# Another order of the first loads and first products in a fused SSM and gated-MLP kernel

## The chip, the cores and the metric

The kernel runs on one core of a Trainium2 chip. The metric is the device time of one execution in microseconds (us); lower is better.

## The reference

The input x has 2048 rows of 512 values. Each row is normalised (layer norm without scale or shift), and the normalised rows `xn` go into two branches whose results are added to x:

```python
xn = _layernorm(x, axis=-1)
return x + _A_ref(xn, ...) + _B_ref(xn, w1, w3, w2)

# A: a diagonal state-space model with 512 complex states, a scan over the 2048 rows
Bu = einsum("bld,pd->blp", x + 0j, B_bar)
h = Lam_bar * h + Bu[:, t, :]                      # for each row t
y = 2.0 * einsum("blp,dp->bld", hseq, Cmat).real + x * Dskip
# B: a gated MLP with 1792 hidden values
out = (silu(x @ w1) * (x @ w3)) @ w2
```

Inputs and output are bf16. The change touches only how the first 512 rows get into branch B.

## The kernel before

Rows are worked in four blocks of 512 (`x_blk[0..3]`), each with four row tiles of 128 (called c = 0..3 in block 0). TensorE needs xn with the features on partitions, `xnT[b]`: 4 feature tiles of 128 (`NDT` = 4; `H` = 2 is one half of the contraction) by 512 rows. For later blocks VectorE normalises and a DMA transposes. Block 0 goes another way, since everything waits for it: VectorE takes mean and variance (`stats`, L164, `aggr`, L167), ScalarE makes the reciprocal root (`rstd_act`, L171 and L172), VectorE normalises (`normed`, L192), TensorE transposes 128x128 pieces against an identity into PSUM (`turn`, L251), and ScalarE or VectorE copies them out (`put`, L256 and L258).

The MLP's first layer has 14 column tiles f of 128 for w1 and for w3. `glu_mm` (L372) multiplies one f tile by some rows over some of the four contraction tiles `dts`. For f = 0, 1, 2 of block 0 the products begin piecewise, as soon as pieces of xnT and of the weights are there: `ahead` (called at L533 to L551) writes them into the three pairs of PSUM tiles `begun`, for rows `c` to `c+n` and the contraction half `lo` or `hi`. The rest of the layer is `glu_up`. Then come the state-space inputs (`ssm_in`, L411) and the outputs (`y_out`, L488 and L493).

The order of instructions on every engine is the order in which the program writes them. Other work of VectorE is drained from a queue with a cost for each task; it lies behind the stretch that the change touches.

DMAs are issued by SyncE and by ScalarE, each on a ring of its own. Completion semaphores are handed out to the DMAs from eight in turn, and an issue that takes a used one waits until the DMA before it on that semaphore has landed. SyncE issues, in this order: rows 0 to 127, rows 128 to 255 (L77), then w1 and w3 for f = 0 to 3, each in two contraction halves of 256 KB (L95, by `load_w13(0, 4, 2)`), then larger pieces. ScalarE issues Lambda_re (L109), rows 256 to 511 (L77), Lambda_im and log_dt, 1 KB each except for the rows. The three small vectors land in `prm`, which VectorE clears first, and TensorE transposes it (L544) for `par_cols`.

`keep_warm` (L150) issues products of constants that nobody reads, into a PSUM tile that is later overwritten.

Of the kernel before, what the change touches and what calls it, by code (L numbers as in the profile page):

```python
# [16 lines left out]
P = 128  # L17
# [3 lines left out]
def kernel(  # L21
# [24 lines left out]
    nc = tc.nc  # L46
# [6 lines left out]
    CPB = TBLK // P  # L53
    NSB = TBLK // SB
    NDT = D // P
# [20 lines left out]
    def load_rows(c0, c1, eng):  # L76
        eng.dma_start(out=x_blk[0][:, c0:c1, :], in_=xv[:, 0, c0:c1, :])  # L77
# [4 lines left out]
    w1_sb = const.tile([P, NDT, F], BF16, name="w1_sb")  # L82
    w3_sb = const.tile([P, NDT, F], BF16, name="w3_sb")
    w2_sb = const.tile([P, NFT, D], BF16, name="w2_sb")
    w1v = B_w1.rearrange("(t p) f -> p t f", p=P)
    w3v = B_w3.rearrange("(t p) f -> p t f", p=P)

    H = NDT // 2

    def load_w13(f0, f1, parts=1):  # L90
        fs = slice(f0 * P, f1 * P)
        for w_sb, wv in ((w1_sb, w1v), (w3_sb, w3v)):
            for i in range(parts):
                ds = slice(i * NDT // parts, (i + 1) * NDT // parts)
                nc.sync.dma_start(out=w_sb[:, ds, fs], in_=wv[:, ds, fs])  # L95

    dskip_row = const.tile([P, D], BF16, name="dskip_row")
    bt = [const.tile([P, NDT, PS], BF16, name=f"bt{ri}") for ri in range(2)]
# [9 lines left out]
    def load_prm(i, src, eng):  # L108
        eng.dma_start(out=prm[i * NPT:(i + 1) * NPT, :], in_=src.rearrange("(t p) -> t p", p=P))  # L109

    load_prm(0, A_Lambda_re, nc.scalar)
    load_rows(2, CPB, nc.scalar)
    load_prm(1, A_Lambda_im, nc.scalar)
    load_prm(2, A_log_dt, nc.scalar)
    load_w13(0, 4, 2)
    load_w13(4, 8)
    nc.sync.dma_start(out=x_blk[1], in_=xv[:, 1, :, :])
    load_w13(8, NFT)
    nc.sync.dma_start(out=dskip_row, in_=A_Dskip.partition_broadcast(P))
    load_turned(bt[0], A_B_re)  # L120
# [26 lines left out]
    def keep_warm(n, width=512):  # L147
        one = nc.const_aps.tensor_like(1.0, like=ident[:, 0:1])
        for _ in range(n):
            nc.tensor.matmul(out=begun[0][0][:, :width], lhsT=one.to_broadcast([P, P]), rhs=one.to_broadcast([P, width]),  # L150
                             start=True, stop=True)

    keep_warm(8)
    keep_warm(5, P)


    mv_all = const.tile([P, NBLK * CPB, 2], FP32, name="mv_all")
# [4 lines left out]
    def stats(c):  # L162
        sums[c] = work.tile([P, 6], FP32, name="stats", bufs=4)
        nc.vector.bn_stats(out=sums[c], in_=x_blk[c // CPB][:, c % CPB, :])  # L164
# [4 lines left out]
    def rstd_act(c0, c1):  # L169
        y = rstd_all[:, c0:c1]  # L170
        nc.scalar.activation(out=y, in_=mv_all[:, c0:c1, 1], func=ACT.Ln, bias=LN_EPS)  # L171
        nc.scalar.activation(out=y, in_=y, func=ACT.Exp, scale=-0.5)  # L172
# [15 lines left out]
    def normed(c, parts=1):  # L188
        xn = work.tile([P, D], BF16, name="xn", bufs=8)
        for i in range(parts):  # L190
            ds = slice(i * D // parts, (i + 1) * D // parts)
            nc.vector.tensor_scalar(out=xn[:, ds], in0=x_blk[c // CPB][:, c % CPB, ds], scalar1=mv_all[:, c, 0:1],  # L192
                                    scalar2=rstd_all[:, c:c + 1], op0=ALU.subtract, op1=ALU.mult)
        return xn
# [54 lines left out]
    def turn(c, pxt, d0=0, d1=NDT):  # L249
        for dt in range(d0, d1):  # L250
            nc.tensor.transpose(out=pxt[:, dt - d0, :], in_=xn0[c][:, dt * P:(dt + 1) * P], identity=ident)  # L251

    def put(c, pxt, eng, d0=0, d1=NDT):
        dst = xnTs[0][:, d0:d1, c * P:(c + 1) * P]
        if eng is nc.scalar:
            nc.scalar.activation(out=dst, in_=pxt, func=ACT.Copy)  # L256
        else:
            nc.vector.tensor_copy(out=dst, in_=pxt)  # L258
# [110 lines left out]
    def glu_mm(b, f, w_sb, ps, ts, dts=range(NDT), joins=False):  # L369

        for dt in dts:
            nc.tensor.matmul(out=ps[:, ts], lhsT=w_sb[:, dt, f * P:(f + 1) * P], rhs=xnTs[b][:, dt, ts],  # L372
                             start=(dt == 0 and not joins), stop=(dt == NDT - 1))
# [128 lines left out]
    def ahead(w_sbs, fs, c, n=1, dts=range(NDT), joins=False):  # L502
        for f in fs:
            for w_sb in w_sbs:
                glu_mm(0, f, w_sb, begun[f][w_sb is w3_sb], slice(c * P, (c + n) * P), dts, joins)
# [13 lines left out]
    xn0[1] = normed(1, 2)  # L519
    turn(0, tb, H, NDT)  # L520
    put(0, tb, nc.scalar, H, NDT)
    keep_warm(2, P)
    turn(1, t1[0], 0, H)
    put(1, t1[0], nc.scalar, 0, H)
    turn(1, t1[1], H, NDT)
    put(1, t1[1], nc.scalar, H, NDT)
    stats(2)
    aggr(2)
    rstd_act(2, 3)
    stats(3)  # L530
    B3 = (0, 1, 2)
    lo, hi = range(H), range(H, NDT)
    ahead((w1_sb,), B3, 0, 1, lo)  # L533
    ahead((w1_sb,), B3, 1, 1, lo, True)
    ahead((w1_sb,), B3, 0, 2, hi)
    xn0[2] = normed(2)
    aggr(3)
    rstd_act(3, 4)
    ahead((w3_sb,), B3, 0, 2, lo)
    turn(2, t2)  # L540
    put(2, t2, nc.vector)
    xn0[3] = normed(3)
    ahead((w3_sb,), B3, 0, 2, hi)
    nc.tensor.transpose(out=pprm, in_=prm, identity=ident)  # L544
# [63 lines left out]
```

## Time and profile before

| | us |
|---|---|
| median of 3 runs | 211.74 (211.68 to 211.76) |
| the profiled execution | 212.11 |
| its span, first to last instruction | 210.3 |
| TensorE busy in the span | 206.6 (98%) |
| VectorE busy | 173.5 (82%) |
| ScalarE busy | 93.4 (44%) |

The span is what the profile's views show; the rest of the profiled execution's time lies around it. Times in the views are counted from the start of the span. A TensorE row's duration reaches to the modelled end of the product, so that of two rows in sequence the first seems to run into the second; the starts tell the pace. In the rows PE is TensorE, PEld its weight load, DVE VectorE, ACT ScalarE, POOL GpSimd and SP SyncE.

### The profile page before, as it was taken

The numbers are of one execution on the slowest core, as the hardware profiler recorded it, in microseconds if no ns is written. First come the engines' busy times: TensorE is split into PE (matmuls) and PEld (weight loads), VectorE is DVE, ScalarE is ACT, GpSimd is POOL, SyncE is SP. The second block draws the span as 40 slices with busy tenths as digits, with TensorE's granted clock in tenths as the row PEclk, the third lists the DMA queues.
The fourth block names the chain that finished last, engine by engine and source line by source line (L and its number), as shares of the span: only waits on it lengthen the run. The fifth ranks groups of instructions, "written<-read, shape, count | busy, mean of one in ns | idle before, by whom it ended". The sixth has DMA issues, their size and how long they took to land.

```text
span 210.3 us, 2878 instructions
## 1 busy us (share of the span) xinstructions
PE 206.6 (98%) x1036; PEld 97.7 (46%) x1036; DVE 173.5 (82%) x346; ACT 93.4 (44%) x167; POOL 6.0 (3%) x27
## 2 busy tenths in 40 slices
PE   8999999999999999999999999999999999999994
PEld 3864444444444444444444444444444444444453
DVE  4699989989999999999999999999999999121111
ACT  3599967666666200066666600036666620000000
POOL 2010320000000000000000000000000000000000
PEclk9999999999999999999999999999999999999999
DMA  5999599944000000000004200100000000000110
GB/s 165 294 366 219 109 178 325 217 106 100 0 3 0 0 25 25 28 26 0 0 0 77 28 1 24 50 25 5 0 0 0 0 3 25 27 25 25 34 44 25
DMA packets 25014, 13.69 MB, mean 65 GB/s; under 512 B 15912, under 2 KB 25000, under 8 KB 25000
## 3 DMA queue, kind: packets, MB, share of 16 engines
q1 hardware_dynamic: 24704, 13.24, 26.1%
q10 hardware_dynamic: 296, 0.27, 0.4%
q8 instruction: 8, 0.13, 0.3%
q14 instruction: 6, 0.05, 0.1%
HBM read 7.74 MB, written 2.10 MB: 47 GB/s over the span
## 4 chain that ended last, share of the span: by engine, by line
PE 96%; DMA 2%; SPq 0%; DVE 0%; issue 0%
PE g_ps L372 23%; PE u_ps L372 23%; PE y_ps L488 23%; PE y_ps L493 13%; PE bu_ps L411 13%; DMA w_sb<-in_B_w_dram 2%; SPq L77 0%; PE xt_ps L251 0%; DVE o L498 0%; PE xt_ps L544 0%
## 5 line engine op out<-in xcount | busy, mean ns | idle before, releaser
L372 PEld LDWEIGHTS <-w_sb 128*128 128x128 bf16 x502 | 46.4, 98 | 50.6 <-DMA w_sb<-in_B_w_dram 0.6
L372 PE MATMUL g_ps<-xnT,w_sb 128*128 128x512 bf16 (+2 forms) x254 | 58.2, 354 | 0.3 <-DMA w_sb<-in_B_w_dram 0.3
L372 PE MATMUL u_ps<-xnT,w_sb 128*128 128x512 bf16 (+2 forms) x248 | 58.4, 358 | 0.0
L488 PE MATMUL y_ps<-w_sb,hgT 128*128 128x512 bf16 (+2 forms) x238 | 51.2, 366 | 0.0
L390 ACT ACTIVATE up<-u_ps 128x512 bf16<-128x512 f32 x56 | 34.0, 607 | 14.9 <-PE u_ps L372 14.9
L413 ACT ACTIVATE u<-bu_ps 128x512 bf16<-128x512 f32 x32 | 19.1, 597 | 46.3 <-PE bu_ps L411 46.3
L388 ACT ACTIVATE sl<-g_ps 128x512 bf16<-128x512 f32 x56 | 34.0, 608 | 9.9 <-PE g_ps L372 9.2
L445 DVE TENSOR_TENSOR_SCAN ab<-r_col,h,ab 128x256 bf16<-128x256 f32 x56 | 37.7, 733 | 0.2
L488 PEld LDWEIGHTS <-hgT 128*128 128x128 bf16 x238 | 22.8, 98 | 25.9
L498 DVE TENSOR_TENSOR o<-y_ps,x_blk 128x512 bf16<-128x512 f32 (+2 forms) x17 | 11.1, 654 | 24.3 <-PE y_ps L493 24.3
L493 PE MATMUL y_ps<-ct,h 128*128 128x512 bf16 (+2 forms) x136 | 30.4, 366 | 0.0
L411 PE MATMUL bu_ps<-xnT,bt 128*128 128x512 bf16 x128 | 28.1, 379 | 0.0
L397 DVE TENSOR_TENSOR hgT<-sl,up 128x512 bf16<-128x512 bf16 x56 | 22.9, 414 | 2.1 <-ACT up L390 2.1
L493 PEld LDWEIGHTS <-h 128*128 128x128 bf16 x136 | 13.0, 98 | 14.7
L411 PEld LDWEIGHTS <-bt 128*128 128x128 bf16 x128 | 12.5, 98 | 15.1
L164 DVE BATCH_NORM_STATS2 stats<-x_blk 128x6 f32<-128x512 bf16 x16 | 10.6, 675 | 2.5 <-DMA x_blk<-in_A_x_dram 2.5
L454 DVE TENSOR_TENSOR ab<-ab,tab_s 128x2048 bf16<-128x2048 bf16 x8 | 9.8, 1222 | 0.2
L450 DVE TENSOR_TENSOR ab<-ab,tab_c 128x2048 bf16<-128x2048 bf16 x8 | 9.8, 1222 | 0.1
L427 DVE TENSOR_TENSOR ab<-u,tab_x 128x2048 bf16<-128x2048 bf16 x8 | 9.7, 1219 | 0.0
L430 DVE TENSOR_TENSOR ab<-u,tab_y 128x2048 bf16<-128x2048 bf16 x8 | 9.7, 1218 | 0.0
L201 DVE TENSOR_TENSOR x_blk<-xd,x_blk 128x512 bf16<-128x512 bf16 x16 | 6.8, 426 | 0.5
L200 DVE TENSOR_TENSOR xd<-xn,dskip_row 128x512 bf16<-128x512 bf16 x16 | 6.7, 418 | 0.0
(76 smaller groups left out, 81.3 us busy)
## 6 DMA issues: line engine op xcount, KB each, us to landing
out_dram<-o SPq DMA_DIRECT2D x15, 128.0 KB, 1.7
w_sb<-in_B_w_dram SPq DMA_DIRECT2D x1, 1792.0 KB, 9.3
x_blk<-in_A_x_dram SPq DMA_DIRECT2D x3, 512.0 KB, 6.3
w_sb<-in_B_w_dram SPq DMA_DIRECT2D x2, 768.0 KB, 7.8
w_sb<-in_B_w_dram SPq DMA_DIRECT2D x4, 256.0 KB, 5.0
w_sb<-in_B_w_dram SPq DMA_DIRECT2D x2, 512.0 KB, 4.1
x_blk<-in_A_x_dram SPq DMA_DIRECT2D x2, 128.0 KB, 2.2
x_blk<-in_A_x_dram ACTq DMA_DIRECT2D x1, 256.0 KB, 4.7
```

What stands on the lines that cost most here:

```text
L164: nc.vector.bn_stats(out=sums[c], in_=x_blk[c // CPB][:, c % CPB, :])
L372: nc.tensor.matmul(out=ps[:, ts], lhsT=w_sb[:, dt, f * P:(f + 1) * P], rhs=xnTs[b][:, dt, ts], start=(dt == 0 and not joins), stop=(dt == ...
L388: nc.scalar.activation(out=sl16, in_=g_ps, func=ACT.Silu)
L390: nc.scalar.activation(out=up16, in_=u_ps, func=ACT.Copy)
L397: nc.vector.tensor_tensor(out=hg[b][:, f, :], in0=sl16, in1=up16, op=ALU.mult)
L411: nc.tensor.matmul(out=u_ps, lhsT=bt[ri][:, dt, pt * P:(pt + 1) * P], rhs=xnTs[b][:, dt, :], start=(dt == 0), stop=(dt == NDT - 1))
L413: nc.scalar.activation(out=u16[:, :, pt, ri, :], in_=u_ps.rearrange("p (s t) -> p s t", s=NSB), func=ACT.Copy)
L445: nc.vector.tensor_tensor_scan(out=a[:, pt, 2 * ri + 1, :], data0=r_b, data1=a[:, pt, 2 * ri, :], initial=init, op0=ALU.mult, op1=ALU.add)
L450: nc.vector.tensor_tensor(out=a[:, :, 0::2, :], in0=a[:, :, 1::2, :], in1=tab_b("c"), op=ALU.mult)
L488: nc.tensor.matmul(out=y_ps[:, ds], lhsT=hg[b][:, f, cl * P:(cl + 1) * P], rhs=w2_sb[:, f, ds], start=(f == 0), stop=False)
L493: nc.tensor.matmul(out=y_ps[:, ds], lhsT=h_tiles[i][:, pt, ri, h_ts], rhs=ct[ri][:, pt, ds], start=False, stop=(pt == NPT - 1 and ri == 1))
L498: nc.vector.tensor_tensor(out=o16[:, ds], in0=y_ps[:, ds], in1=x_blk[b][:, cl, ds], op=ALU.add)
```

## The change

Three things are changed, all in the first 8 us.

The loads: on ScalarE's ring rows 256 to 511 are issued first, and Lambda_re and Lambda_im behind them. `load_w13` loses its parts, and a helper `load_w` issues the same four halves of w1 and w3 in the same order on SyncE.

The dummies: five narrow ones become seven.

The first products: before, the products of w1 came behind both halves of row tile 1's transposition, for all three f tiles: rows of tile 0 and then of tile 1 by the lower half, then both together by the upper half. After, four products of row tile 0 by the lower half (f = 0, 1) stand between the two halves of row tile 1's transposition; behind it follow row tile 0 by the upper half, row tile 1 by the lower and by the upper half, all for f = 0, 1, and then f = 2 for both row tiles with the whole contraction. The number of columns multiplied is the same.

```diff
-    def load_w13(f0, f1, parts=1):
+    def load_w(w_sb, wv, f0, f1, eng, ds=slice(0, NDT)):
         fs = slice(f0 * P, f1 * P)
-        for w_sb, wv in ((w1_sb, w1v), (w3_sb, w3v)):
-            for i in range(parts):
-                ds = slice(i * NDT // parts, (i + 1) * NDT // parts)
-                nc.sync.dma_start(out=w_sb[:, ds, fs], in_=wv[:, ds, fs])
+        eng.dma_start(out=w_sb[:, ds, fs], in_=wv[:, ds, fs])
+
+    def load_w13(f0, f1):
+        load_w(w1_sb, w1v, f0, f1, nc.sync)
+        load_w(w3_sb, w3v, f0, f1, nc.sync)
...
+    low, high = slice(0, H), slice(H, NDT)
+    load_rows(2, CPB, nc.scalar)
     load_prm(0, A_Lambda_re, nc.scalar)
-    load_rows(2, CPB, nc.scalar)
     load_prm(1, A_Lambda_im, nc.scalar)
+    load_w(w1_sb, w1v, 0, 4, nc.sync, low)
+    load_w(w1_sb, w1v, 0, 4, nc.sync, high)
     load_prm(2, A_log_dt, nc.scalar)
-    load_w13(0, 4, 2)
+    load_w(w3_sb, w3v, 0, 4, nc.sync, low)
+    load_w(w3_sb, w3v, 0, 4, nc.sync, high)
     load_w13(4, 8)
...
     keep_warm(8)
-    keep_warm(5, P)
+    keep_warm(7, P)
...
     xn0[1] = normed(1, 2)
     turn(0, tb, H, NDT)
     put(0, tb, nc.scalar, H, NDT)
+    B3 = (0, 1, 2)
+    lo, hi = range(H), range(H, NDT)
     keep_warm(2, P)
     turn(1, t1[0], 0, H)
     put(1, t1[0], nc.scalar, 0, H)
+    ahead((w1_sb,), (0, 1), 0, 1, lo)
     turn(1, t1[1], H, NDT)
     put(1, t1[1], nc.scalar, H, NDT)
     stats(2)
     aggr(2)
     rstd_act(2, 3)
     stats(3)
-    B3 = (0, 1, 2)
-    lo, hi = range(H), range(H, NDT)
-    ahead((w1_sb,), B3, 0, 1, lo)
-    ahead((w1_sb,), B3, 1, 1, lo, True)
-    ahead((w1_sb,), B3, 0, 2, hi)
+    ahead((w1_sb,), (0, 1), 0, 1, hi)
+    ahead((w1_sb,), (0, 1), 1, 1, lo)
+    ahead((w1_sb,), (0, 1), 1, 1, hi)
+    ahead((w1_sb,), (2,), 0, 2)
     xn0[2] = normed(2)
```

## The prediction, made before the changed kernel was run

> **What bounds the kernel now.** I read the page first, then the chain of waits in order of time, then the opening on TensorE, ScalarE, VectorE and the DMA engines. The page gives the bound:
>
> ```profile
> span 210.3 us, 2878 instructions
> ...
> PE 206.6 (98%) x1036; PEld 97.7 (46%) x1036; DVE 173.5 (82%) x346; ACT 93.4 (44%) x167; POOL 6.0 (3%) x27
> ...
> PE 96%; DMA 2%; SPq 0%; DVE 0%; issue 0%
> ```
>
> TensorE carries 96% of the chain, and a DMA 2%. The chain in order of time says where that DMA stands: once, at the start.
>
> ```profile
> 1.64 4.80 DMA w_sb<-in_B_w_dram
> 6.43 0.05 issue
> 6.48 1.51 PE g_ps L372 x18
> 7.99 0.67 PE u_ps L372 x6
> ```
>
> From 6.48 us to the last output TensorE is never let wait. A change to the opening can therefore move the end only by moving this stream: if the same products are done d us earlier at some later point, the kernel ends d earlier. I measure it at the first w3 product (the first u_ps row). TensorE's timeline (columns: start, time, engine, line, operation, operands, count, idle time before):
>
> ```profile
> 4.12 0.74 PE L150 MATMUL g_ps<-const-bfloat16-1.0 128*128 128x128 bf16 x5
> 4.88 0.65 PE L251 MATMUL xt_ps<-ident,xn 128*128 128x128 bf16 x4
> 5.33 0.42 PE L150 MATMUL g_ps<-const-bfloat16-1.0 128*128 128x128 bf16 x2
> 5.54 0.42 PE L251 MATMUL g_ps<-ident,xn 128*128 128x128 bf16 x2
> 5.76 0.41 PE L251 MATMUL u_ps<-ident,xn 128*128 128x128 bf16 x2
> 6.48 1.51 PE L372 MATMUL g_ps<-xnT,w_sb 128*128 128x128 bf16 x18 [0.31 <-DMA w_sb<-in_B_w_dram]
> 7.83 0.83 PE L372 MATMUL u_ps<-xnT,w_sb 128*128 128x256 bf16 x6
> ```
>
> The first w3 product starts at 7.83. The idle time is 0.31 us: that is nearly all there is to win. Also seen: pairs at 5.33, 5.54 and 5.76 start 0.21 to 0.22 apart, 0.107 for one of 128 columns; the eighteen products from 6.48 to 7.83 (twelve of 128 columns, six of 256, so 24 units) take 1.35, or 0.056 a unit. Somewhere between 5.9 and 6.48 TensorE doubled its rate, while the granted clock in the windows reads 1.00 throughout.
>
> The copies that supply those products, on ScalarE:
>
> ```profile
> 5.32 0.66 ACT L256 ACTIVATE xnT<-xt_ps 128x256 bf16<-128x256 bf16 x2 [0.25 <-PE xt_ps L251]
> 6.00 0.38 ACT L256 ACTIVATE xnT<-g_ps 128x256 bf16<-128x256 bf16 x1
> 6.28 0.38 ACT L256 ACTIVATE xnT<-u_ps 128x256 bf16<-128x256 bf16 x1
> ```
>
> The last one, the upper half of rows 128 to 255, ends at 6.66. So the path of x is only some 0.2 us behind the weights that TensorE waits for. Both must improve. Last, the DMA engines by stretch (window:length, sums of PE, PEld, DVE, ACT, POOL, granted clock, DMA share, GB/s):
>
> ```profile
> 1.75:3.00 1.25, 1.25 (x5) 0.44 (x3) 0.11 (x1) 0.25 (x1) 0.30 (x1) 1.00 0.89 224
> 3.00:3.75 0.75, 0.75 (x4) 0.20 (x2) 0.72 (x3) 0.00 (x0) 0.00 (x0) 1.00 0.52 93
> 3.75:4.50 0.75, 0.75 (x6) 0.47 (x5) 0.71 (x3) 0.41 (x2) 0.00 (x0) 1.00 0.90 307
> 4.50:7.00 2.50, 2.17 (x24) 1.44 (x22) 1.88 (x7) 1.72 (x6) 0.00 (x0) 1.00 1.08 374
> ```
>
> They move 374 GB/s once busy, but 224 and then 93 at first. The issues by narrow windows, with their time to landing: rows 128 to 255 at 1.17 (2.2), rows 256 to 511 on ScalarE's ring at 1.53 (4.7), w1's lower half at 1.64 (4.8), its upper half at 2.11 (5.0), w3's halves at 2.62 (5.2) and 3.40 (5.0). So weight pieces land at 6.44, 7.11, 7.8 and 8.4, one each 0.68 us, and TensorE uses one in 0.67: behind the first landing, loads and products run at one pace.
>
> **Two dummies more.** Now eight of 512 columns and five of 128 run from 0.76; the last five start at 4.12 and are 0.107 apart, so the array is free at 4.66. Two more: 4.87. The first transposition starts at 4.88. They are hidden if it comes no sooner, and cost nothing.
>
> **The loads' order.** Rows 256 to 511 (256 KB) lose the parameter load ahead of them on ScalarE's ring (0.94 to 1.49) and go at about 0.73, with row block 0, instead of 1.53. The parameters follow at about 1.2 and 1.7, the third after row block 0 as now; all are used at 9.37, so they are free. SyncE's list is the same; its w3 and x loads wait for semaphores that were freed well before. Two effects remain, neither shown by the trace.
>
> Weights earlier, by d. The 256 KB that share the engines with w1 would be gone sooner. If the busy share is what counts, 1.75 to 3.00 has 11% free, 0.14 us. If the bytes are, (374-224)x1.25 = 188 KB fit, and 188/374 = 0.5 us is saved; if the stretch at 93 GB/s also vanishes, (374-93)x0.75/374 = 0.56 more. Ends: 0 (or a little below) and 1.06. I take 0.5: two rings together did reach 374 later.
>
> x later, by a. Blocks 0 and 1 now share with that load. At 374 GB/s, as much again ahead of block 0 (131 KB) is 0.35 us; block 1 is late by up to 0.70, but has slack: it landed at 3.38 and VectorE took it up at 3.71. So a = 0.35 with even sharing at full rate. If all 262 KB go ahead at 224 GB/s, 1.17. If the new load only fills stalls, 0. A gain below zero is excluded: nothing is taken off these two loads but four descriptors. I take 0.3, nearest to the 374 of the only stretch with both rings full. The Trainium skill (DMA: Bandwidth & Descriptors, "Issuing engines are not separate DMA queues") says DMAs from any engine run on the same 16 engines and interleave: by that rule the early start isn't free for blocks 0 and 1, and a is over 0; no row here shows them shared.
>
> **The products' order.** The same columns: before 12 of 128 and 6 of 256, after 16 of 128 and 4 of 256, 24 units either way. But transposition 1's upper half now stands behind four products that wait for w1's first piece, and behind w1's second piece there are now 20 of the units (12 of f=0,1 and 8 of f=2) where there were 12: 20x0.056 = 1.11 us against 0.67. So 0.44 of the weights' gain is given back by order.
>
> **The sum**, with a=0.3 and d=0.5. Lower half of transposition 1 done by 6.06 (5.76+a); its four products need also the copy (5.70+a = 6.00) and w1 (6.48-d = 5.98): start 6.06. Then two transpositions. At 0.056 these six end at 6.39, at 0.107 at 6.70. The copy of the upper half follows 0.26 to 0.35 behind the start of the last transposition (0.35 is 4.97 to 5.32 before): 6.60 to 6.98, or 6.94 to 7.32. w1's second piece is there at 7.16-d = 6.66. f=0,1 of block 0 and the lower half of block 1 run to 7.11 or 7.15; the upper half of block 1 waits for its copy, and starts at 7.11 or 7.34; then 4+8 units, 0.67: first w3 product at 7.78 or 8.01, against 7.83. Change -0.05 to +0.18; middle +0.07. Behind it w3's pieces have 0.5 us more slack, rows 256 to 511 come sooner (VectorE's wait of 0.57 before 6.27 goes; transposition 2 isn't late), the rest moves with TensorE. The profiled execution took 212.11, span 210.3 and 1.8 around it; 212.11+0.07 = 212.18. The median lies 0.37 below it: 211.81.
>
> **Rivals.** A measurement of this kernel can tell about 0.2%, 0.42 us, from no change.
>
> (A) Rows 0 to 255 come late, slower. ScalarE's load, issued at the same moment, runs ahead of both at the slow early rate: a = 1.17. Then block 1's last copy ends at 6.66+1.17 = 7.83, the first w3 product follows 0.69 later at 8.52, and the kernel is at 212.4. It decides from a = 0.9. For: 224 and 93 GB/s show early rates far below full. Against: block 0's descriptors also start at once, on a ring of their own. 0.15.
>
> (B) Weights no earlier (d about 0): w1's second piece at 7.16 and 1.11 behind it, 8.27, so +0.44: 212.2. For: share 0.89 in 1.75 to 3.00 is nearly full. Against: 224 GB/s there. 0.17; half of it is over 0.42.
>
> (C) Both go well, a=0 and d at least 0.8: first product at 5.76, last copy 6.74, w3 at 7.43, so -0.40 at the fast rate, -0.11 at the slow one: 211.35. For: stalls to fill. Against: two things must come together, and the ceiling hardly reaches 0.42. 0.10.
>
> (D) TensorE's rate doubles later: the opening now has waits at 4.9 to 5.2 and in front of w1's pieces. If the doubling took again the 5.7 us that it took at most (0.76 to 6.48), half of that is lost at most, 2.9 us; half as long, 1.4: 213.2. The Trainium skill (TensorE: Matmul & The Clock Gate, "What's actually happening") has a free-running 3.4 us window of activity; by that figure the loss is an estimated 1.7 us. Against: waits of 0.3 us stood there already. 0.04.
>
> **How the numbers follow.** Forecast 0.54, A 0.15, B 0.17, C 0.10, D 0.04. Slower: A 0.13, half of B 0.09, D 0.04, and 0.04 of the forecast. Faster: 0.05 of C beyond what I can price, and 0.05 of the forecast, where both a and d are better than taken and the rate doubles sooner. Within 0.2%: 0.60. Range 211.35 (C) to 212.5 (A with what its price leaves open); its forecast part is 211.5 to 212.1.
>
> **What would show it.** Right: rows 256 to 511 landing near 5 us; VectorE's first statistics at 3.2; first product near 6.1, a second wait in front of w1's upper half or block 1's copy; first w3 product within 0.2 us of 7.83; everything behind it shifted as one. Wrong: statistics at 2.9 with w1 before 5.7 (C), at 3.8 (A), w1 at 6.4 again (B), products 0.107 apart behind 6.5 (D), or a TensorE wait anywhere after 9 us, for which my sum has no term.

## The result: slower by 0.59 us, 0.27%

| | median, us | range | ratio, 95% interval |
|---|---|---|---|
| before (10 runs) | 211.74 | 211.58 to 212.09 | |
| changed (10 runs) | 212.33 | 212.16 to 212.45 | 1.0027 (1.0019 to 1.0035) |

The forecast of 211.81 missed the median by 0.52 us. The time lies in the predicted range of 211.35 to 212.5, but outside the forecast's own part of it (211.5 to 212.1), and on the side that had 0.3, not on the one that had 0.6.

The two profiled executions hide this difference: 212.11 us before, 212.17 after. That of before is slower than each of the ten runs in the table, that of after among the fastest of its own. So a second profile was taken of before and of after, and one of every other kernel below. One relation ties a profile to the timed executions. In nine profiles of kernels that differ only in the opening (before and after twice each, and five of the experiments below), the device time is the start of the first w3 product plus 204.26 to 204.29 us. In the other five (row tile 1 first, and the four with the rows late) TensorE waits again behind that product, and 204.40 or more come on top. The usual execution before (211.74) therefore starts w3 at about 7.47 us, not at the 7.83 of the profile shown, and the usual one after (212.33) at about 8.06.

From the page of after: the span, the engines, the chain's shares.

```profile
span 210.4 us, 2886 instructions
...
PE 206.0 (98%) x1040; PEld 97.4 (46%) x1040; DVE 173.5 (82%) x346; ACT 93.5 (44%) x167; POOL 6.0 (3%) x27
...
PE 96%; DMA 2%; SPq 1%; DVE 0%; issue 0%
```

The bound and its share are those of before. The opening on TensorE after the change:

```profile
5.20 0.54 PE L256 MATMUL xt_ps<-ident,xn 128*128 128x128 bf16 x4 [0.60 <-DVE xn L197]
...
5.95 0.38 PE L377 MATMUL g_ps<-xnT,w_sb 128*128 128x128 bf16 x4
6.17 0.28 PE L256 MATMUL u_ps<-ident,xn 128*128 128x128 bf16 x2
6.76 1.28 PE L377 MATMUL g_ps<-xnT,w_sb 128*128 128x128 bf16 x16 [0.31 <-DMA w_sb<-in_B_w_dram]
7.88 0.82 PE L377 MATMUL u_ps<-xnT,w_sb 128*128 128x256 bf16 x6
```

The first product starts 0.53 us sooner than in the profile before (5.95 against 6.48), on w1's first half, which landed at 4.76. Then TensorE waits again, 0.31 us, for w1's second half, landed at 6.71. Behind that landing stand 20 units: 6.76 to 7.88 is 1.12 us. Ahead of it, the transposition of block 0 starts at 5.20 instead of 4.88, and waits 0.60 us for VectorE. VectorE's timeline says why:

```profile
2.89 0.69 DVE L169 BATCH_NORM_STATS2 stats<-x_blk 128x6 f32<-128x512 bf16 x1 [1.96 <-DMA x_blk<-in_A_x_dram]
...
3.99 0.69 DVE L169 BATCH_NORM_STATS2 stats<-x_blk 128x6 f32<-128x512 bf16 x1 [0.20 <-DMA x_blk<-in_A_x_dram]
```

The statistics of rows 0 to 127 start as before. Those of rows 128 to 255 wait 0.20 us for their load and start at 3.99, against 3.71; the normalisation of block 0 stands behind them on VectorE, so the delay reaches the first transposition too. The copy that comes last, on ScalarE:

```profile
6.48 0.38 ACT L261 ACTIVATE xnT<-u_ps 128x256 bf16<-128x256 bf16 x1
```

It ends at 6.86, when TensorE has products of row tile 0 by w1's second half to do, so nothing waits for it. The DMA engines in the windows shown before (same columns; last, the share and GB/s):

```profile
1.75:3.00 1.25, 1.25 (x5) 0.44 (x3) 0.11 (x1) 0.25 (x1) 0.30 (x1) 1.00 0.96 288
3.00:3.75 0.75, 0.75 (x4) 0.20 (x2) 0.72 (x2) 0.00 (x0) 0.00 (x0) 1.00 1.01 327
3.75:4.50 0.75, 0.75 (x9) 0.49 (x7) 0.55 (x2) 0.41 (x2) 0.00 (x0) 1.00 1.06 303
4.50:7.00 2.50, 1.58 (x21) 1.05 (x20) 2.42 (x9) 1.89 (x7) 0.00 (x0) 1.00 1.00 299
```

The stall at 93 GB/s is gone, but so is the stretch at 374. The early loads are faster, the later ones slower, and w1's second half lies among the later ones.

Which ring moved the bytes is in the DMA view (queue, packets, MB, share of the 16 engines' time). q10, with 0.27 MB over the whole execution, is ScalarE's ring; q1 is SyncE's. After the change, from 2.50 to 3.00:

```profile
q10 hardware_dynamic: 166, 0.17, 98.4%
q1 hardware_dynamic: 1, 0.00, 0.1%
```

For that half microsecond the early load of rows 256 to 511 had the engines to itself, though rows 128 to 255 had been issued at 1.17. Before, in the same window, SyncE's ring moved 0.11 MB and ScalarE's 0.02.

### The profile page after: what moved, and what is told of

Its sections match the earlier page's. It is cut to its first block, busy times and chain, and to the rows that moved or that the text cites. A ratio compares the mean times of both kernels' runs of the same rounds, so it can differ in the third digit from the quotient of the medians.

```text
span 210.4 us, 2886 instructions
## 1 busy us (share of the span) xinstructions
PE 206.0 (98%) x1040; PEld 97.4 (46%) x1040; DVE 173.5 (82%) x346; ACT 93.5 (44%) x167; POOL 6.0 (3%) x27
## 3 DMA queue, kind: packets, MB, share of 16 engines
HBM read 7.74 MB, written 2.10 MB: 47 GB/s over the span
## 4 chain that ended last, share of the span: by engine, by line
PE 96%; DMA 2%; SPq 1%; DVE 0%; issue 0%
PE u_ps L377 23%; PE g_ps L377 23%; PE y_ps L493 23%; PE y_ps L498 13%; PE bu_ps L416 13%; DMA w_sb<-in_B_w_dram 2%; SPq L77 0%; PE xt_ps L256 0%; SPq L92 0%; DVE o L503 0%; PE xt_ps L551 0%
## 5 line engine op out<-in xcount | busy, mean ns | idle before, releaser
L377 PE MATMUL g_ps<-xnT,w_sb 128*128 128x512 bf16 (+1 forms) x256 | 58.4, 353 | 0.3 <-DMA w_sb<-in_B_w_dram 0.3
```

## The experiments

The theories, by the letters that some expectations use. **X**: x comes late, since rows 256 to 511 now travel beside rows 128 to 255, and the second transposition is held behind products that wait for w1. **W**: the weights decide; w1's second half comes no sooner, and the new order puts more work behind it. **E**: the larger loads issued behind w3 take engines away from w1's second half. **N**: they do not.

**The same code again.** No edit: how far do executions of one kernel differ?

> The kernel before once more, unchanged, for a second profile and for what a comparison of like with like gives. The profile of before took 212.11, 0.37 over its own median. Theory X (late x): in the usual execution w1 lands in time and block 1's last copy (6.66) starts the stream; then this profile should show w1's first half landing by 6.1 rather than 6.43, and the first w3 product near 7.45. Theory W (late weights): the usual execution waits for w1 as the first profile did, w1 at 6.4 and the first w3 product near 7.8; the 0.37 then lies elsewhere. Both: ratio 1.000 within 0.001.

Measured: 211.68 us (ratio 0.9999, 0.9990 to 1.0008). Its profiled execution took 211.57:

```profile
5.68 0.29 PE L251 MATMUL u_ps<-ident,xn 128*128 128x128 bf16 x2
5.80 1.64 PE L372 MATMUL g_ps<-xnT,w_sb 128*128 128x128 bf16 x18
7.28 0.82 PE L372 MATMUL u_ps<-xnT,w_sb 128*128 128x256 bf16 x6
```

Here nothing waits for weights. w1's halves landed at 5.64 and 6.38 instead of 6.43 and 7.11, and the products follow the last transposition at once. The eighteen hide one pause. The two PSUM tiles of f = 2 first hold row tile 1's transposition, so f = 2's first product, the fifth in the old order, waits until the copy has emptied its tile:

```profile
5.75 0.38 ACT L256 ACTIVATE xnT<-g_ps 128x256 bf16<-128x256 bf16 x1
```

The copy ends at 6.13, the fifth product starts at 6.18, and from it on stand 20 units of 128 columns, 1.10 us: w3 at 7.28. In this execution the kernel before is bound by x and its copies. The profile of the dummies alone, at 211.72 a usual execution, has the same chain: copy done at 6.31, w3 at 7.46. The profile used for the prediction was one in which w1 came late.

> The changed kernel once more, unchanged, for a second profile: its first one (span 210.4) stood at the low end of its own executions, whose median is 212.33. In every profile so far the span is the start of the first w3 product plus 202.48, so a usual execution should have it near 8.05. Theory X (late x: rows 128 to 255 held up by the load beside them, and the upper half of transposition 1 held behind products that wait for w1) expects the first transposition at 5.2 to 5.5 and the last wait on a copy, or on w1's halves with the transposition behind it. Theory W (only w1's second half) expects w1's second half to land near 6.9. Median 212.3 in both.

Measured: 212.23 us (1.0031, 1.0014 to 1.0047), and the same picture as in the first profile of after, a little later:

```profile
6.48 0.27 PE L256 MATMUL u_ps<-ident,xn 128*128 128x128 bf16 x2
7.06 1.28 PE L377 MATMUL g_ps<-xnT,w_sb 128*128 128x128 bf16 x16 [0.30 <-DMA w_sb<-in_B_w_dram]
8.17 0.82 PE L377 MATMUL u_ps<-xnT,w_sb 128*128 128x256 bf16 x6
```

w1's second half landed at 7.01, TensorE waited 0.30 us for it, and 1.11 us behind its start comes w3. Both profiles of after are bound by this landing.

**The dummies alone.**

```diff
-    keep_warm(5, P)
+    keep_warm(7, P)
```

> Two more dummies alone. Both theories: the array is free at 4.87 and the first transposition is ready at 4.88, so no difference, within 0.1. If the difference of 0.59 comes from the dummies, 212.3.

Measured: 211.70 us (0.9997, 0.9988 to 1.0006). They cost nothing.

**The loads alone**: the order of loads of the change, with the old products and five dummies.

```diff
+    load_rows(2, CPB, nc.scalar)
     load_prm(0, A_Lambda_re, nc.scalar)
-    load_rows(2, CPB, nc.scalar)
     load_prm(1, A_Lambda_im, nc.scalar)
```

> The new order of loads alone, with the old order of products and five dummies. Theory X: a = 0.3 moves block 1's copies from 6.66 to 6.97 and nothing else counts: 0.25 to 0.35 slower than before, 212.05. Theory W: w1 lands 0.4 earlier, the old order gives nothing back, limited by x to a first w3 product at 7.69: 0.14 faster than the first profile, so level with before or up to 0.15 faster, 211.6 to 211.75.

Measured: 212.07 us (1.0017, 1.0008 to 1.0026), 0.38 slower. VectorE and then TensorE:

```profile
4.25 0.69 DVE L169 BATCH_NORM_STATS2 stats<-x_blk 128x6 f32<-128x512 bf16 x1 [0.32 <-DMA x_blk<-in_A_x_dram]
```

```profile
6.44 1.71 PE L377 MATMUL g_ps<-xnT,w_sb 128*128 128x128 bf16 x18
7.99 0.82 PE L377 MATMUL u_ps<-xnT,w_sb 128*128 128x256 bf16 x6
```

The second statistics wait 0.32 us and start at 4.25, 0.54 behind the 3.71 of before. The first product starts behind the last transposition (6.32), though w1's first half landed at 6.07, and the fifth waits for the copy of row tile 1's lower half, which ends at 6.84; it starts at 6.89, and 1.10 later comes w3. So the loads cost time by the path of x, as X says.

**The products alone**: the new order of products with the old loads and five dummies.

```diff
+    ahead((w1_sb,), (0, 1), 0, 1, lo)
     turn(1, t1[1], H, NDT)
...
-    ahead((w1_sb,), B3, 0, 1, lo)
-    ahead((w1_sb,), B3, 1, 1, lo, True)
-    ahead((w1_sb,), B3, 0, 2, hi)
+    ahead((w1_sb,), (0, 1), 0, 1, hi)
+    ahead((w1_sb,), (0, 1), 1, 1, lo)
+    ahead((w1_sb,), (0, 1), 1, 1, hi)
+    ahead((w1_sb,), (2,), 0, 2)
```

> The new order of products alone, with the old loads and five dummies. Theory X: the upper half of transposition 1 waits for w1 and four products, so block 1's last copy comes 0.2 to 0.4 later: 0.2 to 0.4 slower, 212.0. Theory W: 0.44 more product time behind w1's second half: 0.44 slower, 212.2. The two differ in the profile: in X the wait is on the copy, in W on w1's second half.

Measured: 211.91 us (1.0007, 0.9997 to 1.0017): 0.22 slower by the medians, with no change inside the interval. Its profiled execution (212.27) is at the slow end of its own:

```profile
6.37 0.40 PE L372 MATMUL g_ps<-xnT,w_sb 128*128 128x128 bf16 x4 [0.32 <-DMA w_sb<-in_B_w_dram]
6.61 0.28 PE L251 MATMUL u_ps<-ident,xn 128*128 128x128 bf16 x2
6.80 1.37 PE L372 MATMUL g_ps<-xnT,w_sb 128*128 128x128 bf16 x16
8.01 0.82 PE L372 MATMUL u_ps<-xnT,w_sb 128*128 128x256 bf16 x6
```

The four products wait 0.32 us for w1's first half, and the transposition behind them (6.61) waits with them. Two costs are possible then: that held transposition, or the 20 units behind w1's second half. In this profile both show: the half landed at 6.76, and with 0.05 and 1.11 w3 would start at 7.92; the copy of the held piece ended at 7.30, and the products waited another 0.09 for it. The two medians, 0.38 and 0.22, add up to 0.60, and the whole change costs 0.59; the two costs lie on different paths, so this agreement is no proof (see below).

**No transposition held**: the products alone, but with both halves of row tile 1's transposition ahead of the first four products.

```diff
-    ahead((w1_sb,), (0, 1), 0, 1, lo)
     turn(1, t1[1], H, NDT)
     put(1, t1[1], nc.scalar, H, NDT)
...
+    ahead((w1_sb,), (0, 1), 0, 1, lo)
     ahead((w1_sb,), (0, 1), 0, 1, hi)
```

> The old loads with the new products, but both halves of transposition 1 ahead of them, so that it no longer waits for w1. If the hold is what the new order costs, the loss of products_only (0.22) goes: 211.7, or a little faster, since less has to be there for the first products. If the cost is the 1.11 of product time behind w1's second half against 0.67, it stays: 211.9 to 212.1.

Measured: 211.95 us (1.0015, 1.0007 to 1.0024), 0.22 slower. By the medians the cost is that of the products alone, so holding the transposition is not what costs. What is left of the new order is the amount of work behind w1's second half. The profiled execution shows it, although it is the fastest of its eleven (211.64):

```profile
5.88 1.65 PE L372 MATMUL g_ps<-xnT,w_sb 128*128 128x128 bf16 x20
7.36 0.82 PE L372 MATMUL u_ps<-xnT,w_sb 128*128 128x256 bf16 x6
```

w1's second half landed at 6.20; with the 0.05 us between a landing and the product behind it, and 1.11 for 20 units, that gives 7.36.

**The load moved the other way**: rows 256 to 511 behind all three parameters, so that w1 has the engines to itself for longer; with the old and with the new products.

```diff
-    load_rows(2, CPB, nc.scalar)
     load_prm(1, A_Lambda_im, nc.scalar)
...
     load_prm(2, A_log_dt, nc.scalar)
+    load_rows(2, CPB, nc.scalar)
```

> The kernel before with rows 256 to 511 behind all three parameter loads, so at 3.2 instead of 1.53 (0.74 in the change): the other way along the same line. Theory X: rows 128 to 255 land no sooner than now (3.3), or 0.1 sooner; w1 lands 0.3 to 0.6 sooner since 256 KB no longer share with its first half; the start is then always set by x, first w3 product at 7.28: 211.5, 0.1 to 0.2 faster, with less spread. If what matters is that the DMA engines start full early, everything lands later and it is slower by 0.2 to 0.5. Rows 256 to 511 then land near 6.5, and the third row tile's transposition may come late by 0.1 to 0.2, which would eat the gain.

Measured: 215.06 us (1.0153, 1.0120 to 1.0186), a miss by over 3 us. VectorE, TensorE and the DMA issues (KB each, us to landing):

```profile
9.07 0.70 DVE L164 BATCH_NORM_STATS2 stats<-x_blk 128x6 f32<-128x512 bf16 x1 [3.40 <-DMA x_blk<-in_A_x_dram]
```

```profile
8.86 0.83 PE L372 MATMUL u_ps<-xnT,w_sb 128*128 128x256 bf16 x6 [1.38 <-DMA w_sb<-in_B_w_dram]
```

```profile
x_blk<-in_A_x_dram ACTq DMA_DIRECT2D x1, 256.0 KB, 6.2
```

w1 gained as hoped: its second half landed at 5.34 instead of about 6.6. But the load issued at 2.85 took 6.2 us, w3's first half 6.2 as well, and both are now waited for: w3 for 1.38 us, and the third row tile's transposition, behind the late statistics, for 1.26. The gain on w1 is real and buys nothing. The load hardly moved for two microseconds: from 3.00 to 5.00 ScalarE's ring had 10 of 563 packets, from 5.00 to 7.00 it had 207 of 539.

The 215.06 is also a middle of two kinds. Three of the six executions took 213.75 to 214.40 at a mean granted clock of 1.000, the other three 215.72 to 216.10 at 0.992, among them the profiled one. From its page, the clock in 40 slices of 5.35 us, in tenths of full speed; the 7 is the stretch from 10.7 to 16.1:

```profile
PEclk9979999999999999999999999999999999999999
```

Between 11 and 13 us, behind the two waits, the granted clock is 0.50. By the three executions at 1.000 the late loads cost 2.35 us (214.08 against 211.73).

> rows_later with the new order of products. With w1's first half there by 5.2 the products that stand before the upper half of transposition 1 no longer wait, so the new order should cost nothing (211.5, level with rows_later) or gain up to 0.1, since TensorE has products of block 0 to do while block 1 is copied. If the order itself costs (1.11 against 0.67 behind w1's second half): 0.2 to 0.4 slower than rows_later.

Measured: 214.60 us (1.0144, 1.0107 to 1.0181), also a miss, and by the intervals no different from the one before. TensorE still waits 1.62 us for w3 there. With w3 arriving last, more work behind w1's second half costs nothing that these runs can tell: it lies ahead of that wait.

**The large loads held back**: everything on SyncE's ring behind w3's halves made to wait for a small write of VectorE behind the normalisation of row tile 1; in the changed kernel, and in the two above.

```diff
+    def load_more():
+        nc.vector.memset(w1_sb[:, 0, 4 * P:4 * P + 1], 0.0)
+        load_w13(4, 8)
...
     xn0[1] = normed(1, 2)
+    load_more()
```

> The changed kernel with one more instruction: VectorE clears a column of w1's next piece (f = 4 to 7) behind the second normalisation, so that the 512 KB loads behind the four halves cannot be issued before about 6.0. In the change they go at 4.8 and 5.2, as soon as w1's first half has landed, against 5.5 to 6.4 before. Theory E (early big loads): they take the engines from w1's second half, which lands at 6.7 to 7.0 instead of 6.2 to 6.5; held, it lands by 6.3 and the first w3 product comes at 7.5 to 7.7: 211.8 to 212.0. Theory N: what is issued later on the same ring doesn't hold up what went before, w1's second half stays at 6.7 to 7.0: 212.2 to 212.4.

Measured: 212.12 us (1.0027, 1.0009 to 1.0046), against 1.0031 for the changed kernel in its own series. The large loads are issued from 6.30 instead of from 4.78 and 5.55 (the two profiles of after), and w1's second half still landed at 6.68:

```profile
6.72 1.28 PE L379 MATMUL g_ps<-xnT,w_sb 128*128 128x128 bf16 x16
```

E is not borne out: the large loads went 0.7 to 1.5 us later, and w1's second half came at 6.68 against 6.71 and 7.01, not by 6.3.

> rows_later with the same hold. There the big loads went at 4.7 and 5.1, w3's first half landed at 8.8 and rows 256 to 511, issued at 2.85, at 9.0, and 3.3 us were lost. Theory E: held until 5.8, w3's halves land near 6.1 and 6.8, rows 256 to 511 by 7, and most of the 3.3 comes back: 211.5 to 212.0, level with before or a little faster. Theory N: rows 256 to 511 are late because they were issued late, and w3 because it shares with them: 214 to 215.

> The same with the new order of products. With w1's second half at 5.4 the 1.11 of product time behind it is no bound; if theory E holds for rows_later_held, the new order is level with the old one or up to 0.15 faster: 211.4 to 211.9, which would be the best version here. If theory E fails: 214 to 215 as without the hold.

Measured: 214.40 us (1.0142, 1.0115 to 1.0169) and 213.95 (1.0127, 1.0089 to 1.0164). No difference from the kernels without the hold that the intervals can tell. The held loads still go at 5.74, and w3's first half lands at 8.53 and 8.28 instead of 8.82 and 9.21, so the hold removes at most a part of the lateness. Why a 256 KB load issued at 2.6 to 3.0 needs 5.6 to 6.6 us stayed open. In these four kernels 9 of the 24 executions ran at 0.992.

**Row tile 1 first**: the order of loads again, but rows 128 to 255 go first on ScalarE's ring, and rows 256 to 511 behind rows 0 to 127 on SyncE's.

```diff
-    load_rows(1, 2, nc.sync)
+    load_rows(1, 2, nc.scalar)
...
+    load_rows(2, CPB, nc.sync)
     load_prm(0, A_Lambda_re, nc.scalar)
-    load_rows(2, CPB, nc.scalar)
```

> loads_only with rows 128 to 255 and rows 256 to 511 changing places: block 1 goes first on ScalarE's ring at 0.73, and rows 256 to 511 behind block 0 on SyncE's, at about 1.17, still earlier than before (1.53). Old order of products, five dummies. Theory X (loads_only costs 0.38 because the load beside it holds block 1 up, landing at 4.0 to 4.2 instead of 3.3): block 1 lands at 3.0 to 3.4, the first transposition comes at 4.9, and the 0.38 goes: 211.6 to 211.8, level with before. If the cost lies in when w1 lands, or in that the parameters or anything else is moved, it stays: 212.0 to 212.1.

Measured: 212.41 us (1.0045, 1.0028 to 1.0061), a miss. VectorE's first statistics:

```profile
3.46 0.69 DVE L169 BATCH_NORM_STATS2 stats<-x_blk 128x6 f32<-128x512 bf16 x1 [2.53 <-DMA x_blk<-in_A_x_dram]
```

Row tile 1 was taken up at 4.29 without a wait, but rows 0 to 127, which now travel beside it, came 0.57 us later (3.46 against 2.89). The delay moved from one row tile to the other, and the chain behind it is that of the loads alone: transposition at 5.45, the lower half's copy done at 6.78, w3 at 7.93. In both orders that were tried, a load beside the first rows delays one of them. TensorE then waits once more, for w3's second half, which landed at 8.88 (8.09 in the loads alone); here the device time is 204.40 behind w3.

## Why the prediction was right or wrong

**The bound** was read rightly. The nine profiles show the opening as the only place, and the rest of the program as a constant behind the first w3 product: 204.26 to 204.29 us.

**The base was wrong**, and this is the step that failed most. The prediction added its +0.07 to a profiled execution of 212.11 and took 0.37 off, as if the 0.37 lay somewhere that the change doesn't touch. It lay in the very wait that the change was to win back: w3 at 7.83 there, at 7.47 in the usual execution. Of the 0.52 missed, 0.37 is this base, and the rest the sum's end (7.90 in the middle, against 8.06). That end, a first w3 product between 7.78 and 8.01, came close: the profile after has 7.88. Against 7.47 the same sum reads +0.31 to +0.54, and +0.59 was measured. That the end came close is partly luck. The sum started from w1's second half at 7.11, 0.53 later than the mean of the old loads (below), and took off 0.5 for a gain that didn't come; the two errors nearly cancel. The x path of before, 20 units behind the lower half's copy, isn't in the prediction at all: it compared the weights with the upper half's copy, at 6.66, while the lower half's copy, done at 6.38, gives w3 at 7.53 in that same profile.

**d, the weights' gain, was mis-sized.** It was taken as 0.5 for both halves. Landings, averaged over the profiles with the old loads (five: the two of before, the products alone, the dummies alone, no transposition held) and with the new (four: the two of after, the loads alone, the large loads held back): first half 5.94 and 5.58, so 0.36 earlier; second half 6.58 and 6.79, so 0.2 later. These spread widely (6.20 to 7.11 and 6.68 to 7.01), so a gain of 0.5 is ruled out; that the second half came later isn't shown by the landings alone. An estimate from the medians points that way: behind its landing stand 0.05 + 1.11 in the new order, so the products alone (211.91, w3 at 7.64) can't have it later than 6.48 in a usual execution, while the changed kernel (8.06), if this landing bounds it as in both its profiles, has it at 6.90.

The working of d took the room of 1.75 to 3.75 as a gain for all that follows. Means of the old five against the new three without the hold: 234 and 263 GB/s in 1.75 to 3.00, 180 and 346 in 3.00 to 3.75, 310 and 298 in 3.75 to 4.50, 356 and 286 in 4.50 to 7.00. That is 35 + 125 KB more up to 3.75 and 9 + 174 KB less from there to 7.00. The room was filled, and then lost again. The prediction chose 0.5 because "two rings together did reach 374 later". That reading was wrong; in the profile before, from 5.00 to 7.00, at 375 GB/s:

```profile
q1 hardware_dynamic: 764, 0.74, 106.3%
q10 hardware_dynamic: 27, 0.01, 2.0%
```

One ring alone moved 375 there, and with the rows issued late two busy rings moved 264 in the same window. So the fall isn't for want of a second ring; why the rate falls after the change stays open.

**a, the delay of x,** was 0.3 and is 0.28 to 0.54 by the second statistics, 0.32 to 0.57 by the first transposition. Even sharing gave the right size by the wrong picture: the first statistics didn't move to 3.2 (2.89 and 2.90 in the two profiles of after), and the delay fell on rows 128 to 255, which took 2.8 to 3.0 us to land instead of 2.0 to 2.3. The load of rows 256 to 511 did not share with them, it went ahead of them, 166 packets against 1 from 2.50 to 3.00. Their slack, which the prediction set against it, was used up. Rows 256 to 511 landed at 3.6 to 3.8, not near 5. The Trainium skill's rule (DMA: Bandwidth & Descriptors, "Issuing engines are not separate DMA queues") that loads from two engines interleave on the same DMA engines was the right warning: the trace agrees that the early load isn't free, with 0.8 us more for the load beside it, but the two take turns of half a microsecond here.

**The order's 0.44** is right in size and is what ends last after the change: 1.11 to 1.12 us of products behind w1's second half in every profile bound by it. By itself it costs less, because the usual execution before has room there: 6.58 + 0.05 + 0.67 = 7.30, while x holds w3 until 7.47. With 1.11 it is 7.74, so +0.27 is expected, and 0.22 was measured.

**Dummies and parameters** cost nothing, as said. In both profiles of after everything behind w3 moved as one; no wait of TensorE's behind 9 us was added.

**The rivals.** B, weights no earlier, came true for the half that counts, and is what ends last; its price of 212.2 lies 0.13 below the 212.33. A's 212.4 lies nearer, but by another path: ScalarE's load ran ahead of rows 128 to 255 only, x decides alone where the old products are kept, and there costs half of A's price. Its condition, a at 0.9, was set against the late-w1 execution; where x already bounds, every 0.1 counts. C's sign appeared without its gain: first statistics at 2.9 and w1's first half at 4.76 and 5.53, before 5.7, while the end hung on the second half. D isn't in either profile: TensorE ran at its faster pace well ahead of w1's second half. But one of the twelve executions of after in its second series took 214.26 at a mean clock of 0.992, and one of eleven of the held kernel 214.43 at 0.991, against none below 0.999 in the 84 of before in these series. Neither was profiled, so whether that is D stays open.

So the two parts cost by different paths. The loads alone are late by x (0.38); the products alone by w1's second half (0.22); together, the mean landing of w1's second half with the new loads, 6.79, plus 0.05 and 1.11, gives 7.95, and for the two profiles of after alone (6.86) 8.02, near the 8.06 that the median implies. That 0.38 and 0.22 add up to the whole is then a coincidence: in the new order f = 2 comes last, and in neither profile of after does the end wait for a copy.

## What to carry to other kernels

Ask of a single profile whether it is a usual execution: place its time in the spread of the runs, and if it is at an end, find out which wait makes it so before building a sum on that wait. A load moved earlier takes its share from whatever is urgent at that moment, and room in the early DMA windows isn't a gain for a later load unless the later rate holds. When products are reordered, count what stands behind the last piece to land, not how soon the first product can start.

## What the runs showed of the hardware

Landings scatter between executions of the same code: w1's second half landed at 7.11 and at 6.38 in two executions of before, whose device times were 212.11 and 211.57. A 256 KB load took 2.9 to 6.7 us from issue to landing in these openings. One ring alone kept the DMA engines at 375 GB/s (before, 5.00 to 7.00), and two rings' loads can run one behind the other instead of mixed (after, 2.50 to 3.00).

The time at which TensorE doubles its pace moves too, at a granted clock of 1.00: about 4.0 us in one profile of after and 6.2 in the other, about 4.1 and between 5.9 and 6.48 in the two of before. The four transpositions of row tile 0 take 0.54 us behind it and 0.65 ahead of it. The Trainium skill (TensorE: Matmul & The Clock Gate, "What's actually happening") describes a window that runs free of the program; this scatter agrees with it.

The pace can also fall again: with the rows issued late, behind waits of 1.38 and 1.26 us, the granted clock read 0.50 from 11 to 13 us, and 9 of the 24 executions of those four kernels show such a mean clock of 0.992, though the profiled one of the late rows with the new products waited 1.62 and 1.22 us and stayed at 1.00.
